# A streaming attention decode kernel: wq in two halves, the last unit in one transfer, wo in other parts

## The chip, the cores and the metric

The kernel runs on one core of a Trainium2 chip. The metric is the device time of one execution in microseconds (us), as the median of several runs. TensorE is PE (PEld: its weight loads), VectorE is DVE, ScalarE is ACT, GpSimd is POOL, SyncE is SP. Nearly all transfers are issued by SP, on one queue that 16 DMA engines serve.

## The reference

```python
# x: 2 x 1 x 448;  k_cache, v_cache: 2 x 16 x 4096 x 256;  wq: 448 x 4096;  wo: 4096 x 448
g = sigmoid((x * gate_w).sum(-1, keepdims=True))
q = (x @ wq) as (B, H, 1, Dh)
p = softmax(einsum("bhqd,bhkd->bhqk", q, k_cache) * Dh ** -0.5)
a = einsum("bhqk,bhkd->bhqd", p, v_cache) as (B, 1, H * Dh) @ wo
b = relu(x @ w1) @ w2            # w1: 448 x 1792, w2: 1792 x 448
out = g * a + (1 - g) * b
```

One query token for each of two batch rows, 16 heads, 4096 cached keys: every byte of the two caches (268 MB in float32) is read once.

## The kernel before, in words

The caches are cut into 32 units, one for each pair of batch row and head. A unit is a tile of 128 partitions by 16384 floats (8 MB): its first half holds K, its second V. Three slots of that size (`slot`, in `ring`) hold units in turn, unit u in slot u % 3. The weights pass through the same slots: wq through slot 2 before unit 2 needs it, w1 and w2 through slot 2 and wo through slot 0 when the last units in them are done.

The order of all large transfers is written out by hand in `sync`. SP issues wq, unit 0 and unit 1; then, in a loop of 10 turns of three, it waits for one count of the semaphore `free` (`take`: wait, then subtract) and issues the next unit. PE gives the first count of `free` after both halves of the projection (so that slot 2 may be overwritten), DVE one for each unit that it is done with. The last unit, 31, is issued in two transfers by a branch on the loop's turn: K signals `land[1]`, V signals `late`. After the next two counts come w1 with w2, and wo in 7 transfers of 7, 7, 7, 4, 4, 2 and 1 chunks; a chunk is 128 x 448 floats, and each transfer has its own semaphore. ACT issues one small transfer, xg: x and the gate's weights.

PE (`tensor`) waits for POOL's gate sums and DVE's `sel`, then projects: `project` multiplies 16 tiles into `ph`, ACT scales it into `wide`, PE transposes it into `pt`, ACT copies it into `qt`. It does so twice, one half of wq at a time, written out by a Python loop, after one wait for all of wq. Then for each unit `scores` waits for its landing and for its query, and multiplies K into `ps`. DVE takes the maximum (L284), ACT the exponential (L263) and the next unit's query (L256), DVE multiplies V by the probabilities with an accumulated sum, 8 times (L290). DVE's loop has a branch that waits for `late` in its last turn. In that way PE's scores of one unit run while DVE works on V of the one before.

After unit 31 the tail follows: PE transposes the maxima and sums (L204, L205) and projects with w1 (L172 with `xo`), DVE and ACT make the weights of the softmax (L294 to L298), PE spreads them, DVE scales (L300) and spreads the outputs into `lhs` (L302, semaphore `ot`). PE then multiplies `lhs` with w2's 14 chunks and wo's first 25 into `acc` (L229), waiting for each part of wo where it begins; DVE copies `acc` out (L306), PE folds its four row groups into `z` (L233), and the last 7 chunks (`DIRECT`) are multiplied straight into `z` in four pieces each (L238). DVE copies `z` (L308) and SP sends it.

Of the kernel before, what the change touches and what calls it, by code (L numbers as in the profile page):

```python
# [8 lines left out]
P, HP = 128, 64  # L9
G = 4  # L10
R = P // G
SLOTS = 3
CW = 512
DIRECT = 7


def take(e, sem, n=1):
    e.wait_ge(sem, n)
    e.sem_inc(sem, -n)  # L19
# [7 lines left out]
def gated_mix_decode(nc, xg, kv, wq, w1, w2, wo, out):  # L27
    U, _, LEN = kv.shape
    KC, B = xg.shape[1], xg.shape[2] - 1
    KF = KC - 1  # L30
# [3 lines left out]
    T = DH // P  # L34
    J = DH // R
    S = LEN // (2 * T)
# [6 lines left out]
    RB = R // B  # L43
    NQ = H * DH // (G * CW)
    FG = NF * P // G
    WQ, W1 = wq.shape[1] // NQ, w1.shape[1] // 2
    SCALE = float(DH) ** -0.5
    assert NQ == 2 and U % SLOTS == 2

    def sbuf(name, *shape):  # L50
        return nc.alloc_sbuf_tensor(name, [*shape], F32).ap()
# [2 lines left out]
        return nc.alloc_psum_tensor(name, [P, n], F32).ap()  # L54

    WO = [NF]
    for n in (7, 7, 7, 4, 4, 2, 1):
        WO.append(WO[-1] + n)
    assert WO[-1] == N
    names = ["xg", "wq", "w1", "w2", *(f"wo{k}" for k in WO[1:]), *(f"land{s}" for s in range(SLOTS)), "late",  # L60
             "pool", "vec", "act", "const", "sel", "sums", "gate", "omg", "xo", "proj", "wide", "pt", "hr",
             "query", "score", "top", "prob", "free", "tr", "nb", "e4", "wb", "wp", "os", "po", "ot",
             "acc", "a", "z", "res", "out"]
    sem = {n: nc.alloc_semaphore(n) for n in names}
    land = [sem[f"land{s}"] for s in range(SLOTS)]
# [3 lines left out]
    slot = [ring[:, s * LEN:(s + 1) * LEN] for s in range(SLOTS)]  # L69
# [8 lines left out]
    xr = sbuf("xr", P, KC, R)  # L78
# [23 lines left out]
    def slab(s, lo, hi, rows=slice(0, P)):  # L102
        return ring[rows, s * LEN + lo:s * LEN + hi]

    def rows_of(c, half):
        return slice(0, P) if c < KF else slice(half * HP, (half + 1) * HP)

    def bring(e, dst, src, signal):
        e.dma_start(dst, src).then_inc(signal, 16)  # L109

    def sync(e):
        bring(e, slab(2, 0, NQ * WQ), wq, sem["wq"])
        for u in range(2):
            bring(e, slot[u], kv[u], land[u])
        with e.Fori(0, U // SLOTS) as i:
            for k in range(SLOTS):
                take(e, sem["free"])
                s = (k + 2) % SLOTS
                src = kv[bass.ds(i * SLOTS + (k + 2), 1)].rearrange("o p n -> (o p) n")
                if k < SLOTS - 1:  # L120
                    bring(e, slot[s], src, land[s])
                    continue
                with e.If(i == U // SLOTS - 1):
                    bring(e, slot[s][:, :T * S], src[:, :T * S], land[s])
                    bring(e, slot[s][:, T * S:], src[:, T * S:], sem["late"])
                with e.Else():
                    bring(e, slot[s], src, land[s])
        take(e, sem["free"])
        bring(e, slab(2, 0, W2), w1, sem["w1"])
        bring(e, slab(2, W2, W2 + NF * D), w2, sem["w2"])  # L130
        take(e, sem["free"])
        for lo, hi in zip(WO, WO[1:]):
            bring(e, slab(0, (lo - NF) * D, (hi - NF) * D), wo[:, (lo - NF) * D:(hi - NF) * D], sem[f"wo{hi}"])
        e.wait_ge(sem["res"], 1)
        bring(e, out, res, sem["out"])
        nums = [s.num for n, s in sem.items() if n != "out"]
        assert nums == list(range(nums[0], nums[0] + len(nums)))
        e.sem_clear(range(nums[0], nums[0] + len(nums)))
# [23 lines left out]
    def tensor(e):  # L162
        e.wait_ge(sem["sums"], 1)
        e.matmul(gp, ones, gs, start=True, stop=True).then_inc(sem["gate"], 1)  # L164
        e.wait_ge(sem["sel"], 1)

        def project(x, width, place):
            for c in range(KC):
                for g in range(G):
                    at, half = place(c, g)  # L170
                    r = rows_of(c, half)
                    m = e.matmul(ph[g * R:(g + 1) * R, :width], x[r, c], slab(2, at, at + width, r), start=c == 0,  # L172
                                 stop=c == KC - 1)
            m.then_inc(sem["proj"], 1)
            take(e, sem["wide"])
            for k in range(width // P):
                t = e.transpose(pt[:, k * P:(k + 1) * P], wide[:, k * P:(k + 1) * P], ident)  # L177
            return t

        def scores(s):  # L180
            take(e, land[s], 16)
            take(e, sem["query"])
            for c in range(SG // CW):
                for t in range(T):
                    for g in range(G):
                        at = t * S + g * SG + c * CW
                        m = e.matmul(ps[g * R:(g + 1) * R, c * CW:(c + 1) * CW],  # L187
                                     query[:, t:t + 1].to_broadcast([P, R]), slot[s][:, at:at + CW], start=t == 0,
                                     stop=t == T - 1)
                        if c == SG // CW - 1 and t == T - 1:  # L190
                            m.then_inc(sem["score"], 1)

        e.wait_ge(sem["wq"], 16)
        for i in range(NQ):
            t = project(xr, CW, lambda c, g: (i * WQ + (g * KF + c if c < KF else G * KF + g % 2) * CW, g // 2))
            t.then_inc(sem["pt"], 1)
        e.drain().then_inc(sem["free"], 1)
        with e.Fori(0, -(-U // SLOTS)) as i:
            for s in range(SLOTS - 1):
                scores(s)  # L200
            with e.If(i < U // SLOTS):
                scores(SLOTS - 1)
        take(e, sem["query"])
        e.transpose(tp[:U, :P], nm[:, :U], ident)  # L204
        e.transpose(tp[:U, P:2 * P], ls[:, :U], ident).then_inc(sem["tr"], 1)  # L205
        e.wait_ge(sem["xo"], 1)
        e.wait_ge(sem["w1"], 16)
        project(xo, FG, lambda c, g: (g % 2 * W1 + (g // 2 * KF + c if c < KF else 2 * KF) * FG, g // 2))
        for j in range(2):
            t = e.matmul(pt[j * HP:(j + 1) * HP, KF * P:FG], wide[:, KF * P:FG], ident[:, j * HP:(j + 1) * HP],  # L210
                         start=True, stop=True)
        t.then_inc(sem["pt"], 1)
        e.wait_ge(sem["wb"], 1)
        e.matmul(wp, wb.rearrange("u g r -> u (g r)"), ident[:U, :U], start=True, stop=True).then_inc(sem["wp"], 1)
        e.wait_ge(sem["os"], 1)
        for g in range(G):
            m = e.matmul(po[g * R:(g + 1) * R, :nu], sel, os.rearrange("p u j -> p (u j)")[:, g * nu:(g + 1) * nu],
                         start=True, stop=True)
        m.then_inc(sem["po"], 1)
        e.wait_ge(sem["hr"], 1)  # L220
        e.wait_ge(sem["w2"], 16)
        for k in range(N - DIRECT):
            if k == NF:
                e.wait_ge(sem["ot"], 1)
            if k in WO:
                e.wait_ge(sem[f"wo{WO[WO.index(k) + 1]}"], 16)
            g = k % G
            w = slab(2, W2 + k * D, W2 + (k + 1) * D) if k < NF else slab(0, (k - NF) * D, (k - NF + 1) * D)
            m = e.matmul(acc[g * R:(g + 1) * R], lhs[:, k], w, start=k < G, stop=k >= N - DIRECT - G)  # L229
        m.then_inc(sem["acc"], 1)  # L230
        e.wait_ge(sem["a"], 1)
        for g in range(G):
            e.matmul(z[g * R:(g + 1) * R], sel, a_sb[:, g * DG:(g + 1) * DG], start=True, stop=False)  # L233
        for k in range(N - DIRECT, N):
            if k in WO:
                e.wait_ge(sem[f"wo{WO[WO.index(k) + 1]}"], 16)
            for g in range(G):
                m = e.matmul(z[g * R:(g + 1) * R], lhs[:, k], slab(0, (k - NF) * D + g * DG, (k - NF) * D + (g + 1) * DG),  # L238
                             start=False, stop=k == N - 1)
        m.then_inc(sem["z"], 1)  # L240
# [38 lines left out]
    def vector(e):  # L279
        e.wait_ge(sem["const"], 1)  # L280
        e.tensor_reduce(sel, ident.rearrange("p (g r) -> p r g", g=G), axis=AX.X, op=ALU.add).then_inc(sem["sel"], 1)  # L281
        with e.Fori(0, U) as u:
            take(e, sem["score"], G)
            e.tensor_reduce(nm[:, bass.ds(u, 1)], ps, axis=AX.X, op=ALU.max, negate=True).then_inc(sem["top"], 1)  # L284
            take(e, sem["prob"])
            with e.If(u == U - 1):
                e.wait_ge(sem["late"], 16)
            for j in range(J):
                v = ring[:, bass.ds((u % SLOTS) * LEN + (T * S + j * SG), SG)]
                m = e.scalar_tensor_tensor(v, v, 1.0, prob, op0=ALU.mult, op1=ALU.mult,  # L290
                                           accum_out=ov[:, bass.ds(u, 1), j])
            m.then_inc(sem["free"], 1)
# [77 lines left out]
```

## Time and profile before

| what | us |
|---|---|
| median of 3 runs (lowest, highest) | 675.61 (675.5, 675.85) |
| the profiled execution | 675.75 |
| its span, first to last instruction | 674.4 |
| DVE busy in the span | 338.8 |
| PE busy in the span | 213.4 |
| ACT busy in the span | 60.1 |
| DMA engines, share of the span | 99.3% of 16 |
| bytes read | 289.54 MB, 429 GB/s over the span |

The span is what the timeline counts, from 0; the execution's time is 1.35 us more. The page divides the span into 40 slices of 16.9 us; in its rows a digit is a busy share in tenths. In a timeline row stand the start, the duration, the engine, the line, the operation, output and inputs, how many instructions were merged, and in brackets how long the engine was idle before and what ended that. `PEq L19`, `DVEq L19` or `ACTq L19` there means a wait in `take`. In a row of windows stand the stretch, its length, each engine's busy time with its count of instructions, the clock that PE was granted, the share of the DMA engines and their GB/s.

### The profile page before, as it was taken

Reading aid. Unit: us, or ns where it says so; the run is one execution under the profiler, and the core shown is the slowest. Engines: PE = TensorE matmul, PEld = TensorE weight load, DVE = VectorE, ACT = ScalarE, POOL = GpSimd, SP = SyncE. Lnnn points to the kernel's source line nnn. Section 1 sums busy time; section 2 is a strip of 40 time slices with the busy share of each in tenths; the row PEclk is TensorE's granted clock in tenths of the full one; section 3 lists DMA queues with packets and bytes.
Section 4 is the critical chain, followed back from the end, with each engine's and each line's share of the span. In section 5 each row is a group of like instructions: output and inputs, shape, how many; then the busy total and the mean of one; then the engine's idle time right before and its main releaser. Section 6 shows DMA issues by size and latency. Waiting matters only on the chain. (4 is left out here: it accounts for less than half of the span.)

```text
span 674.4 us, 4267 instructions
## 1 busy us (share of the span) xinstructions
PE 213.4 (32%) x1291; PEld 55.9 (8%) x1291; DVE 338.8 (50%) x554; ACT 60.1 (9%) x118; POOL 2.2 (0%) x14
## 2 busy tenths in 40 slices
PE   0633221333332123333321233333222333332455
PEld 0110000000000000000000000000000000000111
DVE  0006566544556664454656545455665544556670
ACT  0020001001000100100010010000001001000110
POOL 0100000000000000000000000000000000000000
PEclk9975567767655676776567676665567667655869
DMA  9999999999999999999999999999999999999997
GB/s 381 428 435 436 435 435 435 435 435 435 435 435 435 435 435 435 435 431 435 435 435 435 435 435 435 435 435 435 435 435 435 435 435 435 435 435 406 414 433 318
DMA packets 6483, 289.65 MB, mean 430 GB/s; under 512 B 976, under 2 KB 1104, under 8 KB 1488
## 3 DMA queue, kind: packets, MB, share of 16 engines
q1 hardware_dynamic: 6336, 289.60, 99.3%
q8 instruction: 3, 0.05, 0.0%
q10 hardware_dynamic: 144, 0.01, 0.0%
HBM read 289.54 MB, written 0.06 MB: 429 GB/s over the span
## 5 line engine op out<-in xcount | busy, mean ns | idle before, releaser
L290 DVE SCALAR_TENSOR_TENSOR ring<-ring,prob 128x1024 f32 x256 | 295.9, 1221 | 78.8 <-DVEq L19 78.8
L187 PE MATMUL ps<-ring,query 128*32 128x512 f32 x1024 | 183.7, 883 | 416.6 <-PEq L19 416.6
L284 DVE TENSOR_REDUCE nm<-ps 128x1024 f32 x32 | 39.2, 1225 | 215.2 <-DVEq L19 215.2
L187 PEld LDWEIGHTS ps<-ring,query 128*32 128x32 f32 x1024 | 46.5, 155 | 553.1 <-issue 553.1
L263 ACT ACTIVATE prob<-ps,nm 128x1024 f32<-128x1024 f32 x32 | 35.6, 1113 | 370.9 <-ACTq L19 370.7
L263 ACT ACT_TABLE_LOAD x11 | 14.1, 1283 | 180.3 <-ACTq L19 180.3
L290 DVE DVE_READ_ACCUMULATOR ring<-ring,prob x256 | 21.2, 83 | 0.0
L281 DVE TENSOR_REDUCE sel<-ident 128x32 f32<-128x128 f32 x1 | 0.4, 369 | 22.7 <-POOL ident L155 22.7
L229 PE MATMUL acc<-ring,lhs 128*32 128x448 f32 x78 | 9.2, 544 | 4.9 <-DMA ring<-in_wo 4.9
L172 PE MATMUL ph<-ring,xr 128*32 128x512 f32 (+1 forms) x64 | 9.2, 713 | 0.7 <-DVE sel L281 0.7
L164 PE MATMUL tp<-gs,ones 128*128 128x2 f32 x2 | 0.6, 364 | 21.8 <-POOL gs L150 21.8
L306 DVE COPY wide<-acc 128x448 f32<-128x448 f32 x1 | 0.6, 625 | 12.7 <-PE acc L229 12.7
L172 PE MATMUL ph<-ring,xo 128*32 128x448 f32 (+1 forms) x32 | 5.4, 826 | 3.8 <-DMA ring<-in_w 3.8
L256 ACT ACTIVATE query<-qt 128x2 f32 (+1 forms) x33 | 6.4, 193 | 0.0
L263 ACT ACTIVATION_READ_ACCUMULATOR prob<-ps,nm x32 | 6.2, 193 | 0.0
L229 PEld LDWEIGHTS acc<-ring,lhs 128*32 128x32 f32 x78 | 2.5, 109 | 10.8 <-DMA ring<-in_wo 7.3
L177 PE MATMUL pt<-ident,wide 128*128 128x128 f32 x11 | 1.8, 280 | 2.7 <-PEq L19 2.7
L204 PE MATMUL tp<-ident,nm 128*32 128x128 f32 x1 | 0.4, 370 | 7.1 <-PEq L19 7.1
L172 PEld LDWEIGHTS ph<-ring,xr 128*32 128x32 f32 (+1 forms) x64 | 1.9, 126 | 6.5 <-issue 5.7
L164 PEld LDWEIGHTS tp<-gs,ones 128*128 128x128 f32 x2 | 0.5, 312 | 21.8 <-POOL gs L150 21.8
L249 ACT ACTIVATE wide<-ph 128x512 f32<-128x512 f32 x2 | 1.2, 597 | 9.6 <-ACTq L19 9.6
L238 PE MATMUL z<-ring,lhs 128*32 128x112 f32 x56 | 1.9, 264 | 0.1
(43 smaller groups left out, 15.2 us busy)
## 6 DMA issues: line engine op xcount, KB each, us to landing
ring<-in_kv SPq DMA_DIRECT2D x2, 4096.0 KB, 33.5
ring<-in_wq SPq DMA_DIRECT2D x1, 7168.0 KB, 19.6
ring<-in_w SPq DMA_DIRECT2D x2, 3136.0 KB, 29.9
ring<-in_wo SPq DMA_DIRECT2D x3, 1568.0 KB, 21.9
ring<-in_wo SPq DMA_DIRECT2D x2, 896.0 KB, 27.7
ring<-in_kv SPq DMA_DIRECT2D x31, 38.3
ring<-in_wo SPq DMA_DIRECT2D x1, 448.0 KB, 29.1
ring<-in_wo SPq DMA_DIRECT2D x1, 224.0 KB, 29.2
```

Of the source, the lines that this page charges most:

```text
L164: e.matmul(gp, ones, gs, start=True, stop=True).then_inc(sem["gate"], 1)
L172: m = e.matmul(ph[g * R:(g + 1) * R, :width], x[r, c], slab(2, at, at + width, r), start=c == 0, stop=c == KC - 1)
L177: t = e.transpose(pt[:, k * P:(k + 1) * P], wide[:, k * P:(k + 1) * P], ident)
L187: m = e.matmul(ps[g * R:(g + 1) * R, c * CW:(c + 1) * CW], query[:, t:t + 1].to_broadcast([P, R]), slot[s][:, at:at + CW], start=t == 0, s ...
L229: m = e.matmul(acc[g * R:(g + 1) * R], lhs[:, k], w, start=k < G, stop=k >= N - DIRECT - G)
L238: m = e.matmul(z[g * R:(g + 1) * R], lhs[:, k], slab(0, (k - NF) * D + g * DG, (k - NF) * D + (g + 1) * DG), start=False, stop=k == N - 1)
L249: e.activation(wide, ph, AF.Copy, scale=SCALE).then_inc(sem["wide"], 1)
L256: e.activation(query, qt[:, :, bass.ds(u, 1)].rearrange("p t o -> p (t o)"), AF.Copy).then_inc(sem["query"], 1)
L263: e.activation(prob, ps, AF.Exp, bias=nm[:, bass.ds(u, 1)], accum_out=ls[:, bass.ds(u, 1)]).then_inc(sem["prob"], 1)
L284: e.tensor_reduce(nm[:, bass.ds(u, 1)], ps, axis=AX.X, op=ALU.max, negate=True).then_inc(sem["top"], 1)
L290: m = e.scalar_tensor_tensor(v, v, 1.0, prob, op0=ALU.mult, op1=ALU.mult, accum_out=ov[:, bass.ds(u, 1), j])
L306: e.tensor_copy(a_sb, acc).then_inc(sem["a"], 1)
```

## The change

wq arrives as an array of two halves. Both are brought to the same place in slot 2: the first before unit 0, the second, after a count of `free`, before unit 1. PE's two projections become a loop of two turns on the chip, each of which waits for its half and gives a count of `free` after a drain. The last unit comes in one transfer like all others, so the branch in SP's loop, the branch in DVE's loop and the semaphore `late` go. wo comes in parts of 9, 9, 5, 3, 3, 2 and 1 chunks, of which the last 6 chunks, not 7, go straight into `z`.

```diff
-DIRECT = 7
+DIRECT = 6
...
-    WQ, W1 = wq.shape[1] // NQ, w1.shape[1] // 2
+    WQ, W1 = wq.shape[2], w1.shape[1] // 2
...
-    for n in (7, 7, 7, 4, 4, 2, 1):
+    for n in (9, 9, 5, 3, 3, 2, 1):
...
     def sync(e):
-        bring(e, slab(2, 0, NQ * WQ), wq, sem["wq"])
-        for u in range(2):
+        for u in range(NQ):
+            if u:
+                take(e, sem["free"])
+            bring(e, slab(2, 0, WQ), wq[u], sem["wq"])
             bring(e, slot[u], kv[u], land[u])
         with e.Fori(0, U // SLOTS) as i:
             for k in range(SLOTS):
                 take(e, sem["free"])
                 s = (k + 2) % SLOTS
                 src = kv[bass.ds(i * SLOTS + (k + 2), 1)].rearrange("o p n -> (o p) n")
-                if k < SLOTS - 1:
-                    bring(e, slot[s], src, land[s])
-                    continue
-                with e.If(i == U // SLOTS - 1):
-                    bring(e, slot[s][:, :T * S], src[:, :T * S], land[s])
-                    bring(e, slot[s][:, T * S:], src[:, T * S:], sem["late"])
-                with e.Else():
-                    bring(e, slot[s], src, land[s])
+                bring(e, slot[s], src, land[s])
...
-        e.wait_ge(sem["wq"], 16)
-        for i in range(NQ):
-            t = project(xr, CW, lambda c, g: (i * WQ + (g * KF + c if c < KF else G * KF + g % 2) * CW, g // 2))
+        with e.Fori(0, NQ):
+            take(e, sem["wq"], 16)
+            t = project(xr, CW, lambda c, g: ((g * KF + c if c < KF else G * KF + g % 2) * CW, g // 2))
             t.then_inc(sem["pt"], 1)
-        e.drain().then_inc(sem["free"], 1)
+            e.drain().then_inc(sem["free"], 1)
...
             take(e, sem["prob"])
-            with e.If(u == U - 1):
-                e.wait_ge(sem["late"], 16)
             for j in range(J):
...
-    wq = np.concatenate([full, last], 2).transpose(1, 0, 2).reshape(P, -1)
+    wq = np.concatenate([full, last], 2)
```

More of the change, by code (lines that the diff above doesn't have):

```diff
@@ L56, in gated_mix_decode @@
     WO = [NF]
-    for n in (7, 7, 7, 4, 4, 2, 1):
+    for n in (9, 9, 5, 3, 3, 2, 1):
         WO.append(WO[-1] + n)
     assert WO[-1] == N
-    names = ["xg", "wq", "w1", "w2", *(f"wo{k}" for k in WO[1:]), *(f"land{s}" for s in range(SLOTS)), "late",
+    names = ["xg", "wq", "w1", "w2", *(f"wo{k}" for k in WO[1:]), *(f"land{s}" for s in range(SLOTS)),
              "pool", "vec", "act", "const", "sel", "sums", "gate", "omg", "xo", "proj", "wide", "pt", "hr",
```

## The prediction

> **What bounds the kernel now.** I read the page's first lines first, then the chain that ended last.
>
> ```profile
> span 674.4 us, 4267 instructions
> ...
> DMA  9999999999999999999999999999999999999997
> GB/s 381 428 435 436 435 435 435 435 435 435 435 435 435 435 435 435 435 431 435 435 435 435 435 435 435 435 435 435 435 435 435 435 435 435 435 435 406 414 433 318
> ...
> q1 hardware_dynamic: 6336, 289.60, 99.3%
> q8 instruction: 3, 0.05, 0.0%
> ...
> DMA ring<-in_wo 4%; SPq L109 0%; PE z L238 0%; DVE res L308 0%
> ```
>
> The reader is to see one resource, full from first slice to last. 289.6 MB at 435 GB/s are 665.7 us of the 674.4; what is left is a start, a tail of about 3 us and a few dips. The chain, in order of time, ends with:
>
> ```profile
> 642.27 29.09 DMA ring<-in_wo
> ...
> 671.41 1.00 PE z L238 x24
> ...
> 672.44 0.28 DVE res L308
> ```
>
> So the time is "when does the last byte of wo land", plus 3 us. The change moves no byte out of the stream. It can cost only by (a) letting the queue run dry, or (b) making the last compute later than the last byte; it can gain only at the edges. I go through the places in that order.
>
> **The change at the start.** The timeline of the first 40 us, and two issue rows:
>
> ```profile
> 0.75 0.39 SPq L109 DMA_DIRECT2D ring<-in_wq  x1
> ...
> 20.59 0.20 POOL L146 TENSOR_TENSOR pg<-xg_sb 128x8 f32<-128x8 f32 x1 [19.61 <-DMA xg_sb<-in_xg]
> ...
> 23.15 5.46 PE L172 MATMUL ph<-ring,xr 128*32 128x512 f32 x32 [0.72 <-DVE sel L281]
> ...
> 30.07 3.77 PE L172 MATMUL ph<-ring,xr 128*32 128x512 f32 x32
> ...
> 34.75 0.63 PE L177 MATMUL pt<-ident,wide 128*128 128x128 f32 x4 [0.90 <-PEq L19]
> ...
> 39.93 5.47 PE L187 MATMUL ps<-ring,query 128*32 128x512 f32 x32 [4.56 <-PEq L19]
> ```
>
> ```profile
> ring<-in_wq SPq DMA_DIRECT2D x1, 7168.0 KB, 19.6
> ...
> out<-res SPq DMA_DIRECT2D x1, 56.0 KB, 1.6
> xg_sb<-in_xg ACTq DMA_DIRECT2D x1, 6.0 KB, 19.8
> ```
>
> Now SP issues wq (7168 KB), unit 0 and unit 1 at once. After the change it issues half of wq and unit 0, waits for PE's first turn, then issues the other half and unit 1. Behind that wait stand every later transfer on SP's queue, so the question is whether the order comes before unit 0 has drained. The 6 KB of xg take 19.8 us because they land together with wq, with which they were issued; PE's start (23.15) follows them by 2.6 us. Half of wq is 3.67 MB, 8.4 us less at 435 GB/s, so xg comes at about 12.2 and PE starts at 14.7. A turn took 7.0 us (23.15 to 30.07, where the next begins); turn 1 ends at 21.8. Issue to landing of the smallest transfer is 1.6 us, so the second half can flow by about 23.8. Half of wq and unit 0 have landed at 39.93 less 8.4, 31.5. The margin is some 7 us. If xg came no earlier than today, turn 1 would end at 30.2, the order could flow at 31.8, and the queue would be dry for 0.3 to, counting its own landing delay, 1.1 us. I take 0, as the row that gives 19.8 beside 19.6 ties xg to wq; 1.1 us is kept for the range.
>
> The second half lands when wq and unit 0 had both landed before, at 39.9, since the bytes ahead are the same. Turn 2 takes 7.0 us, to 46.9, and its "free" lets unit 2 be issued, needed only when unit 1 has landed:
>
> ```profile
> 59.26 6.05 PE L187 MATMUL ps<-ring,query 128*32 128x512 f32 x32 [13.85 <-PEq L19]
> 79.57 6.13 PE L187 MATMUL ps<-ring,query 128*32 128x512 f32 x32 [14.27 <-PEq L19]
> 98.88 5.01 PE L187 MATMUL ps<-ring,query 128*32 128x512 f32 x32 [13.18 <-PEq L19]
> ...
> 601.14 6.46 PE L187 MATMUL ps<-ring,query 128*32 128x512 f32 x32 [13.43 <-PEq L19]
> 620.41 5.37 PE L187 MATMUL ps<-ring,query 128*32 128x512 f32 x32 [12.81 <-PEq L19]
> 630.29 5.34 PE L187 MATMUL ps<-ring,query 128*32 128x512 f32 x32 [4.51 <-PEq L19]
> ```
>
> Unit 1 lands at 59.26: 12 us to spare. Unit 0's scores start about 7 us later than now (47 for 39.93). Each unit lands 19.3 us after the last and PE idles 13 to 14 us before each, so the delay is absorbed in one or two units; slot 0 is needed again only when unit 2 has landed (79.57), and unit 0 is done at about 47 + 20. Cost of the two-turn loop, its drain and its wait: 0, covered by those 12 us; without that cover it would be the 7 us of a turn.
>
> **One transfer for the last unit, one branch less.** The bytes and their rate stay: in halves, 8.39 MB of unit 31 and the 3.21 MB of w1 took from 620.41 to 647.08, 435 GB/s, as whole units do. One transfer fewer here and one more for wq cancel. SP's branch goes, unseen behind a queue that is a unit ahead. What changes is when unit 31's compute runs. The tail:
>
> ```profile
> 607.96 1.22 DVE L284 TENSOR_REDUCE nm<-ps 128x1024 f32 x1 [7.40 <-DVEq L19]
> ...
> 611.20 1.23 DVE L290 SCALAR_TENSOR_TENSOR ring<-ring,prob 128x1024 f32 x1 [2.02 <-DVEq L19]
> ...
> 620.37 0.08 DVE L290 DVE_READ_ACCUMULATOR ring<-ring,prob  x1
> ...
> 647.08 5.39 PE L172 MATMUL ph<-ring,xo 128*32 128x448 f32 x32 [3.80 <-DMA ring<-in_w]
> ...
> 652.33 0.14 DVE L294 TENSOR_REDUCE nb<-tp 32x1 f32<-32x4 f32 x1
> ...
> 655.10 4.80 PE L229 MATMUL acc<-ring,lhs 128*32 128x448 f32 x42
> 655.35 1.23 DVE L302 TENSOR_TENSOR lhs<-po,gate 128x1024 f32<-128x1024 f32 x1 [0.44 <-PE po L217]
> ...
> 662.36 1.70 PE L229 MATMUL acc<-ring,lhs 128*32 128x448 f32 x14 [2.45 <-DMA ring<-in_wo]
> ...
> 666.08 1.71 PE L229 MATMUL acc<-ring,lhs 128*32 128x448 f32 x14 [2.02 <-DMA ring<-in_wo]
> ...
> 668.20 0.96 PE L229 MATMUL acc<-ring,lhs 128*32 128x448 f32 x8 [0.41 <-DMA ring<-in_wo]
> ...
> 670.35 2.02 PE L238 MATMUL z<-ring,lhs 128*32 128x112 f32 x56
> ```
>
> Before, unit 31's scores start at 630.29 on its first half and DVE is through at 652.33. After, they wait for the whole unit, 620.41 + 19.3 = 639.7. From the start of scores to DVE's end unit 29 needed 601.14 to 620.37, 19.2 us, with scores of 6.46; scores vary from 5.01 to 6.46, so 17.8 to 19.2. The branch that DVE no longer takes lies in the idle 2.02 ahead of 611.20, of which the exponential and its accumulator read take 1.3; that leaves 0 to 0.5, and I take 0.2. DVE is through at 657.3 to 658.7: **5.0 to 6.4 us later**. Behind it the same steps follow (652.33 to acc's start at 655.10 is 2.8, to the end of L302 at 656.58 is 4.25): acc starts at 660.1 to 661.5, and its wo products may start at 661.6 to 663.0.
>
> Is that still hidden? acc now has 14 w2 chunks and 26 of wo, two instructions each, 80 in all. At full clock 14 instructions took 1.70 with the last one's tail and 8 took 0.96, so one costs about 0.1: 80 take 7.5 to 8 us, and acc could end at 668 to 669.5. The data set their own end: wo flows at 7 chunks in 3.72 us (662.36 to 666.08), 0.53 a chunk, and the last 6 chunks land in the 3.2 us ahead of the end. With the last chunk at about 672.0, as now, the last part of acc (the second 3) lands at 668.8 and is done by 669.5. From the end of acc to the direct products took 1.2 (669.16 to 670.35), and 48 direct instructions cost about 1.1 (56 took 2.02, waits for data included). That gives 671.8; the last chunk's own 8 end at 672.4. So there is slack of 0.6: acc may end at 670.1 unseen. At full clock the later unit is **covered, with about 0.6 us to spare**.
>
> **The clock takes that away.** PE's gap is new: its xo projection, which ended at 652.5, waits for unit 31's query now and so ends about 1.5 us later, near 654; then PE waits for DVE at 657.3 to 658.7 and for ACT behind that: 4 to 4.5 us idle. The trace has such a gap, 625.78 to 630.29:
>
> ```profile
> 624.00:627.00 3.00, 1.78 (x20) 0.28 (x11) 0.87 (x1) 0.00 (x0) 0.00 (x0) 1.00 0.83 360
> 627.00:630.00 3.00, 0.00 (x0) 0.00 (x0) 0.35 (x1) 2.44 (x4) 0.00 (x0) 1.00 1.19 513
> 630.00:633.00 3.00, 2.71 (x16) 0.92 (x20) 2.34 (x5) 0.14 (x2) 0.00 (x0) 0.63 0.81 350
> ```
>
> In these rows the granted clock (third number from the end) falls from 1.00 to 0.63 right after it. What a burst that starts cold costs is read from the scores: 5.01 to 6.46, where the 32 equal instructions at 30.07, in full clock, took 3.77: 1.2 to 2.7 us more. Cold, acc ends at 669.2 to 672.2 instead of 668 to 669.5. Beyond 670.1 each microsecond is one of time: 0 to 1.7 and, at the far corner, 2.1; in the middle 0.3 to 0.6. Warm it is 0. I take +0.3.
>
> The Trainium skill ("TensorE: Matmul & The Clock Gate", Part 1: The HAM clock gate) states that the clock halves after at least one idle window of about 3.4 us and that the windows run free of the kernel. By that rule a gap of 4 to 4.5 us would hold a whole idle window in about a quarter of the phases, so PE would mostly stay warm and the sum would be 0; the row above cooled after a gap of that length, and I give cold the larger weight.
>
> **wo in 9, 9, 5, 3, 3, 2, 1 with six direct.** Seven transfers stay seven, the last two (2, 1) are unchanged, so the tail after the last byte stays: 0. The coarser first parts land later (second at 18 chunks instead of 14), but PE is late anyway and finds both landed. One chunk moved from direct to acc lengthens acc by 0.2 and shortens the direct part by 8 short instructions (0.2); both are in the sums above.
>
> **Sum.** Start 0 (0 to +1.1), last unit and acc +0.3 (0 to +2.1), wo parts 0, instruction blocks (below) 0 (-1.0 to +1.0). The profiled execution took 675.75 us, its span 674.4; the runs' median is 675.61. So 674.4 becomes 674.7, and 675.61 becomes 675.9.
>
> **Rivals.**
> 1. *Cold acc decides outright* (slower). Place: acc, the sum's third term. It passes 0.2% (1.35 us, about what a measurement can tell from no change) when acc ends after 671.5, which needs the late end of both ranges. Time 677.0 to 677.7. For: the 0.63. Against: only the corner of the ranges gets there. 10%.
> 2. *The queue runs dry at the start* (slower). If xg is not earlier, +0.3 to +1.1: 675.9 to 676.7, with the cold acc added up to 677.5. Against: 19.8 beside 19.6. 6%.
> 3. *Instruction blocks move* (faster). The trace has 3 instruction packets, 0.05 MB, some 16 KB each. Scores 1 to 2 stand 20.31 apart where others are 19.31 apart: if each of the 16 engines carries an equal share of a transfer, one that fetches code loses 1.0 us and never catches up. The changed PE program is some 70 instructions shorter (32 matmuls with their loads and 4 transposes with theirs, less a loop). If one packet that now delays the last engine falls behind the last byte, up to 1.0 us is won, if two do, 2.0: 673.6 to 675.2. If two fall on one engine, 1.0 is lost. 16% for the gain, a third of it beyond 1.35 us.
>    The Trainium skill ("Runtime: NRT & Kernel Launch", Instruction fetch mechanics) states that code comes in 16 KiB blocks of 256 instructions and calls a crossing mostly hidden; by it this rival is 0, and the 20.31 is the only row here that speaks against.
> 4. *The change does nothing to the end*: PE stays warm, all cover holds, 675.5 to 675.7. 18%.
>
> **Chances.** The forecast (acc partly cold, 675.6 to 676.9) has 50%. Within 0.2% (674.3 to 677.0) lie the forecast but for its upper edge (47), rival 4 (18), two thirds of rival 3 (11) and half of rival 2 (3): 79%. Slower: rival 1 (10), the rest of rival 2 (3) and the forecast's edge (3): 16%. Faster: the rest of rival 3, 5%. The range 674.7 to 677.2 leaves out the far ends of rivals 1, 2 and 3.
>
> **What would show it.** Right: SP's second wq issue near 22 and no dip below 428 GB/s in the second slice; PE's first projection near 15; unit 31's scores near 639.7; L294 at 657 to 659; a PE clock under 1.00 somewhere in 656 to 666; acc without waits for the first two wo parts; the direct products ending within 1 us of 672.4. Wrong: a dip at 30 us, acc ending after 671.5, or a last wo landing that itself moves by over 0.5 us, which no compute step explains.

## The result and the profile after

The changed kernel's median is 677.11 us (22 runs, 675.61 to 678.10), that of the kernel before 675.79 beside it (22 runs): ratio 1.0017, 95% interval 1.001 to 1.0023. The medians are 1.3 us apart, and the ratio gives 1.2: a loss that is real, but inside the 0.2% that the prediction called no change. The profiled execution took 677.01 us, its span 675.7, 1.3 more than before. The page of the changed kernel (line numbers are those of its own file: L167 projects, L182 scores, L224 is acc, L228 and L233 are z, L287 is nb, L301 res):

```profile
span 675.7 us, 4217 instructions
...
GB/s 404 409 429 435 436 435 435 435 435 435 435 435 435 435 435 435 435 435 435 435 435 435 435 435 435 435 435 435 435 435 435 435 435 435 435 435 435 422 421 287
...
q8 instruction: 2, 0.03, 0.0%
...
PE acc L224 1%; PE z L233 0%; PE pt L172 0%; DVE wide L299 0%; PE tp L209 0%; PE po L212 0%; DVE os L293 0%; PE pt L205 0%; PE z L228 0%; DVE res L301 0%
```

The last line is the answer in short: the chain that ended last no longer holds a transfer. It is PE and DVE from the transposes ahead of the softmax weights (659.55) to the end. Its last part in order of time, and the timeline of the tail:

```profile
661.95 0.44 PE po L212 x8
662.39 9.08 PE acc L224 x80
671.47 0.02 issue
671.49 0.64 DVE wide L299
672.13 0.04 issue
672.17 0.40 PE z L228 x8
672.57 1.20 PE z L233 x48
```

```profile
640.02 5.99 PE L182 MATMUL ps<-ring,query 128*32 128x512 f32 x32 [13.92 <-PEq L19]
...
649.76 5.89 PE L167 MATMUL ph<-ring,xo 128*32 128x448 f32 x32
...
658.59 0.14 DVE L287 TENSOR_REDUCE nb<-tp 32x1 f32<-32x4 f32 x1
...
662.17 9.25 PE L224 MATMUL acc<-ring,lhs 128*32 128x448 f32 x80
```

Unit 31's scores now begin at 640.02 instead of 630.29; DVE is through at 658.59 instead of 652.33; acc is one run of 80 products with no wait for wo, from 662.17 to 671.47, where before it had waits in it and ended at 669.16. In windows, the clock (third number from the end) says what acc ran at:

```profile
652.00:655.00 3.00, 3.00 (x20) 0.59 (x16) 3.00 (x5) 0.00 (x0) 0.00 (x0) 0.50 0.98 420
655.00:658.00 3.00, 0.66 (x8) 0.00 (x0) 3.00 (x7) 0.00 (x0) 0.00 (x0) 0.99 1.00 430
658.00:661.00 3.00, 1.41 (x8) 0.99 (x9) 1.32 (x7) 0.68 (x2) 0.00 (x0) 0.58 1.00 430
661.00:664.00 3.00, 2.49 (x22) 1.10 (x26) 1.65 (x2) 0.55 (x1) 0.00 (x0) 0.50 0.96 406
664.00:667.00 3.00, 3.00 (x28) 0.87 (x24) 0.00 (x0) 0.00 (x0) 0.00 (x0) 0.78 1.00 415
667.00:670.00 3.00, 3.00 (x36) 0.96 (x32) 0.00 (x0) 0.00 (x0) 0.00 (x0) 1.00 1.00 406
```

PE had just come to full clock at 655 when its work ran out (the xo projection ends at 655.65), and when it resumed at 659.59 it was at 0.50 again, until about 665.

At the start, nothing was lost:

```profile
14.94 6.34 PE L167 MATMUL ph<-ring,xr 128*32 128x512 f32 x32 [0.91 <-PEq L19]
...
39.87 5.83 PE L167 MATMUL ph<-ring,xr 128*32 128x512 f32 x32 [17.07 <-PEq L19]
...
59.32 6.21 PE L182 MATMUL ps<-ring,query 128*32 128x512 f32 x32 [7.56 <-PEq L19]
78.81 5.01 PE L182 MATMUL ps<-ring,query 128*32 128x512 f32 x32 [13.28 <-PEq L19]
99.19 5.06 PE L182 MATMUL ps<-ring,query 128*32 128x512 f32 x32 [15.37 <-PEq L19]
```

```profile
22.95 0.33 SPq L109 DMA_DIRECT2D ring<-in_wq  x1
```

```profile
xg_sb<-in_xg ACTq DMA_DIRECT2D x1, 6.0 KB, 11.4
```

Unit 1 lands where it did (59.32 for 59.26), so the queue was never dry. One step between units is a microsecond too long. Before it stood between 59.26 and 79.57 (20.31 us), now between 78.81 and 99.19 (20.38): it came one unit later, and the trace's records of the instruction packet moved with it, from 63.0 to 82.6, which fits a program that is shorter ahead of PE's loop.

### The profile page after: what moved, and what is told of

The parts are those of the page before. It is cut to its first block, busy times and chain, and to the rows that moved or that the text cites. A ratio compares the mean times of both kernels' runs of the same rounds, so it can differ in the third digit from the quotient of the medians.

```text
span 675.7 us, 4217 instructions
## 1 busy us (share of the span) xinstructions
PE 216.7 (32%) x1285; PEld 57.2 (8%) x1285; DVE 338.9 (50%) x554; ACT 60.1 (9%) x118; POOL 2.2 (0%) x14
## 5 line engine op out<-in xcount | busy, mean ns | idle before, releaser
L182 PE MATMUL ps<-ring,query 128*32 128x512 f32 x1024 | 183.5, 882 | 415.3 <-PEq L19 415.3
L182 PEld LDWEIGHTS ps<-ring,query 128*32 128x32 f32 x1024 | 46.5, 155 | 551.6 <-issue 551.6
L167 PE MATMUL ph<-ring,xr 128*32 128x512 f32 (+1 forms) x64 | 12.2, 911 | 18.0 <-PEq L19 18.0
L224 PE MATMUL acc<-ring,lhs 128*32 128x448 f32 x80 | 9.2, 625 | 0.0
L167 PE MATMUL ph<-ring,xo 128*32 128x448 f32 (+1 forms) x32 | 5.9, 891 | 0.0
L167 PEld LDWEIGHTS ph<-ring,xr 128*32 128x32 f32 (+1 forms) x64 | 2.6, 150 | 26.1 <-issue 26.1
L224 PEld LDWEIGHTS acc<-ring,lhs 128*32 128x32 f32 x80 | 2.8, 128 | 5.8 <-issue 5.8
L167 PEld LDWEIGHTS ph<-ring,xo 128*32 128x32 f32 (+1 forms) x32 | 1.2, 158 | 4.1 <-issue 4.1
```

The costliest lines, as they stand in the source:

```text
L182: m = e.matmul(ps[g * R:(g + 1) * R, c * CW:(c + 1) * CW], query[:, t:t + 1].to_broadcast([P, R]), slot[s][:, at:at + CW], start=t == 0, s ...
```

## The experiments

Theory: unit 31's compute, moved 6 us later by the single transfer, uncovers the tail, and PE's gap before acc, which costs it its clock, does the rest. Rivals: the start (S), the coarser wo parts (W), lateness alone without the clock (L). All runs are timed beside the kernel before (675.65 to 675.88 in the four sets).

**1. The changed kernel, unit 31 in two transfers again.**

```diff
+                if k < SLOTS - 1:
+                    bring(e, slot[s], src, land[s])
+                    continue
+                with e.If(i == U // SLOTS - 1):
+                    bring(e, slot[s][:, :T * S], src[:, :T * S], land[s])
+                    bring(e, slot[s][:, T * S:], src[:, T * S:], sem["late"])
+                with e.Else():
+                    bring(e, slot[s], src, land[s])
...
+            with e.If(u == U - 1):
+                e.wait_ge(sem["late"], 16)
```

> The changed kernel with unit 31 in two transfers again (both branches and late are back); wq in halves and wo in 9, 9, 5, 3, 3, 2, 1 stay. Theory (unit 31 is computed 6 us later and its acc runs partly at half clock): all of the loss goes, 675.6 to 675.9, the chain ends in the transfer of wo again, and acc starts near 655. Rival W (the coarser wo parts cost it) and rival S (the start does): 676.9 to 677.3, as the changed kernel.

675.61 us (11 runs, 675.30 to 675.90), ratio 0.9993 (0.9984 to 1.0002). The whole loss is gone, acc starts at 655.30, and as the start and the wo parts are still changed here, neither S nor W can hold it.

**2. The kernel before, with unit 31 in one transfer** (the same lines the other way).

> The kernel before with unit 31 in one transfer and without both branches; wq whole, wo in 7, 7, 7, 4, 4, 2, 1. Theory: the whole loss is here, 676.5 to 677.5, and the chain ends in acc on PE. Rivals W and S: 675.6 to 675.9.

677.25 us (676.13 to 677.80), ratio 1.0018 (1.0009 to 1.0027). This part alone makes the whole loss; the chain ends in acc on PE.

**3. The changed kernel with the old wo parts** (7, 7, 7, 4, 4, 2, 1 and DIRECT = 7).

> The changed kernel with wo in 7, 7, 7, 4, 4, 2, 1 and seven direct chunks. Theory: acc ends 0.2 to 0.4 us earlier (one chunk less) and the direct part is one chunk longer, so within 0.2 us of the changed kernel, 676.8 to 677.3. Rival W: 675.7, as before.

677.69 us (676.35 to 678.23), ratio 1.0021 (1.0012 to 1.003). No better than the changed kernel, a little above the expected band, and its interval overlaps the changed kernel's. W fails here.

**4. The changed kernel with PE kept busy in the gap.**

```diff
-        def project(x, width, place):
+        def project(x, width, place, fill=0):
...
             m.then_inc(sem["proj"], 1)
+            for f in range(fill):
+                g = f % G
+                e.matmul(ps[g * R:(g + 1) * R, :CW], query[:, :1].to_broadcast([P, R]), slot[1][:, :CW], start=True,
+                         stop=True)
...
+        project(xo, FG, lambda c, g: (g % 2 * W1 + (g // 2 * KF + c if c < KF else 2 * KF) * FG, g // 2), fill=13)
```

> The changed kernel with 13 products of no use on PE between the xo projection and its transposes, into a bank that is read no more, so that PE is busy for 2.8 us (at full clock) of its 3.9 us of waiting for DVE. Theory: PE keeps full clock, acc ends at about 669.5 instead of 671.5 though it starts no earlier, 675.6 to 676.0, and the spread of single runs (675.6 to 678.1 in the changed kernel) shrinks to under 1 us. Rival L (the lateness alone does it, the clock does not matter): 676.9 to 677.3. If the projection itself ends cold, the products take up to 5.5 us and cost up to 1.6 us in some runs.

676.08 us (675.62 to 677.09), ratio 0.9999 (0.9981 to 1.0017). That interval is wide and overlaps the changed kernel's (1.001 to 1.0023). The runs of the same set are clearer: 10 of the 11 of experiment 3 are above 676.7, 9 of the 11 here are at 676.6 or below. Windows of this run, and rows of its timeline:

```profile
655.00:658.00 3.00, 3.00 (x32) 0.79 (x25) 3.00 (x7) 0.00 (x0) 0.00 (x0) 1.00 1.00 430
658.00:661.00 3.00, 2.14 (x15) 0.91 (x10) 1.54 (x8) 1.22 (x3) 0.00 (x0) 1.00 1.00 430
661.00:664.00 3.00, 2.96 (x40) 1.28 (x44) 1.23 (x1) 0.00 (x0) 0.00 (x0) 1.00 0.99 422
```

```profile
655.40 3.62 PE L172 MATMUL ps<-ring,query 128*32 128x512 f32 x26
...
658.40 0.14 DVE L291 TENSOR_REDUCE nb<-tp 32x1 f32<-32x4 f32 x1
...
661.17 8.41 PE L228 MATMUL acc<-ring,lhs 128*32 128x448 f32 x80
...
670.53 1.71 PE L237 MATMUL z<-ring,lhs 128*32 128x112 f32 x48
```

DVE is only 0.2 us earlier than in the changed kernel (658.40 for 658.59), yet acc begins 1.0 us earlier: the other 0.8 come from the small products ahead of it, which run at full clock too. acc takes 8.41, its waits for wo included, for 9.25, and ends at 669.58, inside the 670.1 that the prediction allowed. So L fails: adding useless work took away about 1 us, and the loss needs both, the lateness and the clock.

Two limits. The useless products also make PE's program 52 instructions longer, and this run has 3 instruction packets where the changed kernel has 2. Length is not what gained the time in the trace, as the changed kernel's chain holds no transfer and its out took 1.6 us; but no run put the same instructions elsewhere. And the spread (1.5 us) shrank less than expected. By the packet records the third packet ends at 673.3, 0.2 us ahead of the first bytes of out, so the longer runs may have met what experiment 8 shows below; none of them was traced.

**5. The start alone** (the kernel before with wq in halves and the loop of two turns).

> The kernel before with the start alone changed: wq in two halves into one place, PE in a loop of two turns; unit 31 in two transfers, wo in 7, 7, 7, 4, 4, 2, 1. Theory (the loss is the late unit 31 and its acc at half clock): 675.6 to 675.9, second order for wq near 23 us. A rival that holds part of the loss at the start: 676.1 or more.

675.91 us (675.51 to 677.50, two of 11 runs at 677.5), ratio 1.0002 (0.9993 to 1.0011). No cost; S fails. What the two runs met is open.

**6. DVE later: the changed kernel with two more passes after unit 31.**

```diff
+        for j in range(2):
+            v = ring[:, LEN + j * SG:LEN + (j + 1) * SG]
+            e.scalar_tensor_tensor(v, v, 1.0, prob, op0=ALU.mult, op1=ALU.mult, accum_out=res[:, j:j + 1])
         e.wait_ge(sem["tr"], 1)
```

> The changed kernel with two more passes on DVE after unit 31's, over K that is read no more, their sums unused: DVE reaches L287 2.3 us later. Theory: past the slack every microsecond counts, and PE's gap of 6.2 us now always holds a whole idle window, so the time is 2.3 us above the slower runs of the changed kernel: 679.0 to 680.0, spread under 1.5 us. Rival (something other than the late end of unit 31 sets the loss, and acc has cover left): 677.0 to 678.0.

680.38 us (5 runs, 679.11 to 681.26), ratio 1.0067 (1.0053 to 1.0081): 3.3 us over the changed kernel for 2.3 us of work. There is no cover left, as expected. Size and spread came out above the band, and acc took longer (9.84 for 9.25). PE's gap was 6.19 us and its clock did fall in it; that such a gap always cools PE is more than one trace shows.

```profile
664.43 9.84 PE L224 MATMUL acc<-ring,lhs 128*32 128x448 f32 x80
```

**7. DVE earlier: the changed kernel with 4 passes over V for unit 31** (`attend(U - 1, ..., J // 2)` behind the loop, which now runs to U - 1). It leaves out half of unit 31's output, so it stands for the time alone.

> The changed kernel with 4 instead of 8 passes over V for unit 31 (half of that unit's output is left out and filled from unit 30); the last unit still comes in one transfer, with the changed start and wo parts. DVE reaches L287 4.5 us earlier, near 654. Theory: it is the lateness, not the form of the transfer: 675.5 to 675.9, chain back in the transfer of wo. Rival (the single transfer itself is slower, or hurts what comes behind it): 676.8 to 677.3.

675.57 us (675.36 to 676.20), ratio 0.9999 (0.999 to 1.0008). With the transfer still in one piece and DVE through at 654.15 instead of 658.59, the loss is gone. The form of the transfer costs nothing; what waits for it does.

**8. The wo parts alone, twice, and what follows from them** (the kernel before with 9, 9, 5, 3, 3, 2, 1 and six direct chunks).

> The kernel before with wo alone in 9, 9, 5, 3, 3, 2, 1 and six direct chunks. Theory: 675.6 to 675.9, acc waits for its parts and PE may lose its clock between them, but acc ends by 670. A rival that holds part of the loss in the coarser parts: 676.1 or more.

> The kernel before with wo alone in 9, 9, 5, 3, 3, 2, 1, a second time and beside the next one. If the cost of the parts is real: 676.3 to 677.0 with single runs up to 677.6. If the first time was chance: 675.6 to 675.9.

676.67 us (675.47 to 677.63), ratio 1.0013 (1.0004 to 1.0022), and again 676.13 (675.37 to 677.48), ratio 1.0008 (0.9999 to 1.0017). A miss: here the parts do cost, in some runs, by 1 to 2 us. Beside the second of these, experiment 1's kernel, which has the same parts, ran once more:

> The changed kernel with unit 31 in two transfers, a second time: it has the same coarse parts and was 675.61. If the coarse parts cost in every such kernel, this time some runs come out at 676.5 to 677.6; if the changed start protects it, 675.5 to 675.8 again.

675.59 us (675.40 to 676.00), ratio 1.0 (0.9991 to 1.0009). So it is not the parts as such. My first guess was the clock again, now in the gaps between the coarser parts, and I filled them:

```diff
         for k in range(N - DIRECT):
             if k == NF:
                 e.wait_ge(sem["ot"], 1)
+            for f in range({NF: 7, WO[1]: 8}.get(k, 0)):
+                e.matmul(ps[f % G * R:(f % G + 1) * R, :CW], query[:, :1].to_broadcast([P, R]), slot[1][:, :CW],
+                         start=True, stop=True)
```

> The kernel before with wo in 9, 9, 5, 3, 3, 2, 1 and six direct chunks (676.67 alone), and 7 and 8 products of no use on PE ahead of its waits for the first two parts, which fill most of its gaps of 1.9 and 2.3 us there. Theory C (the coarser parts cost through the clock: a gap of 2.3 us in a window of 3.4 us lets PE fall to half clock in some runs, and the rest of acc is late): 675.6 to 675.9, no run above 676.5 but those that the kernel before has too. Rival F (the cost of the coarser parts lies elsewhere, in the transfers or the code fetch): as without them, 676.3 to 677.0.

675.63 us (675.35 to 676.04), ratio 0.9997 (0.9988 to 1.0006): as theory C said. But the profile of the second run of the wo parts had caught one of its long executions (677.24 us), and it speaks against C. Its windows of the tail, its order for out, its instruction packets with out's time to landing, and the same two rows of the first run's profile (an execution of 675.83 us):

```profile
660.00:663.00 3.00, 2.54 (x26) 1.10 (x18) 0.00 (x0) 0.00 (x0) 0.00 (x0) 1.00 0.95 406
663.00:666.00 3.00, 1.34 (x16) 0.53 (x17) 0.00 (x0) 0.00 (x0) 0.00 (x0) 1.00 1.00 419
666.00:669.00 3.00, 2.77 (x19) 0.57 (x17) 0.00 (x0) 0.00 (x0) 0.00 (x0) 1.00 1.01 418
669.00:672.00 3.00, 2.24 (x55) 1.15 (x54) 0.62 (x1) 0.00 (x0) 0.00 (x0) 1.00 0.36 140
```

```profile
672.94 0.35 SPq L109 DMA_DIRECT2D out<-res  x1
```

```profile
q8 instruction: 3, 0.05, 0.0%
...
out<-res SPq DMA_DIRECT2D x1, 56.0 KB, 3.0
```

```profile
q8 instruction: 2, 0.03, 0.0%
...
out<-res SPq DMA_DIRECT2D x1, 56.0 KB, 1.6
```

The clock is 1.00 in these rows and out is issued at 672.94, within 0.4 us of the short executions (from 655 to 661 the clock was 0.70 and 0.73, but acc then waits 2.12 us for wo, and the short execution of the last run below was as cold there). It is out itself that takes 3.0 us instead of 1.6, in the execution that has a third instruction packet. In the trace's packet records that packet runs from 673.63 to 674.86, just ahead of the bytes of out, and the last packets of out begin at 674.84; in the kernel before it begins at 671.6, and the shorter execution has none. The fill of theory C had also made PE's program 60 instructions longer, so its result did not tell the two apart. The last run has the longer program without the fill near the end:

```diff
         e.drain().then_inc(sem["free"], 1)
+        for f in range(15):
+            e.matmul(ps[f % G * R:(f % G + 1) * R, :P], ones[:, :R], ident, start=True, stop=True)
         with e.Fori(0, -(-U // SLOTS)) as i:
```

> The kernel before with wo alone in 9, 9, 5, 3, 3, 2, 1 and six direct chunks (676.67 and 676.13 alone), and 15 products of no use at 36 us, where PE waits for unit 0: they lengthen PE's program by 60 instructions, as the products of the run with PE kept busy between the parts did (675.63), but do nothing to PE's clock near the end. Theory B (an instruction packet that comes only after the last byte of wo stands in front of the 56 KB of out in some runs, 3.0 us for 1.6; a longer program asks for it earlier): 675.5 to 675.9, no run above 676.5, three instruction packets. Theory C (the clock between the coarser parts): 676.1 to 676.7 with runs up to 677.5, as without the padding.

675.64 us (675.22 to 676.16), ratio 0.9997 (0.9988 to 1.0006), three instruction packets, out in 1.6 us, no run above 676.2. The clock from 655 to 661 was 0.61 and 0.82. The longer program also moved the first packet, from 63.0 to 46.0, and the step that is a microsecond too long went with it (units at 40.01 and 60.20, 20.19 us apart).

Theory B is borne out: that loss was a matter of program length, not of the parts. The profiles fit it. The kernels with a PE program at least as long as the kernel before (experiment 2 and the two padded ones) have 3 packets; the parts alone, 12 instructions shorter, have 2 in one execution and 3 in the other; the changed kernel and experiments 1, 3, 5, 6 and 7, shortened by the loop, have 2. Experiment 4, with the loop and 52 instructions more, has 3, the last one late (672.3). The changed kernel does not show the loss in its profiled execution (out in 1.6 us). What stays open is that only one long execution was traced, and that the last run was timed without the unpadded kernel beside it.

No version beat the kernel before by more than its interval; the best (experiment 1 and the two padded kernels of experiment 8) are level with it.

## Why the prediction was right or wrong, point by point

- *The bound and the direction*: right. The end is the last byte of wo plus 3 us unless a late compute passes it; here it did.
- *The forecast and rival 1*: by its time the result is rival 1's and not the forecast's. The 677.11 lies in its 677.0 to 677.7 (10%) and above the 675.6 to 676.9 that had 50%, and acc ended at 671.47, at the edge of the 671.5 that rival 1 named. That the loss still stayed within 0.2% (0.17), and the median 0.1 us inside the range, is in part luck.
- *Start, 0*: right, by experiments 1 and 5. xg came when half of wq did (PE's first projection at 14.94, foretold 14.7), SP's second order at 22.95, against a need at 31.5. One of the signs that I named was badly chosen: the second slice fell to 409 GB/s, below the 428 that I had set, while the first rose from 381 to 404; unit 1's landing shows that nothing was dry. Rival 2 did not come.
- *Unit 31 later by 5.0 to 6.4 us*: right, 658.59 less 652.33 is 6.26, near the late end, with scores of 5.99. The last bytes of wo did not move (671.6 by the packet records, before and after), but the direct products ended at 673.72, 1.3 past the 672.4 that I had named as a sign.
- *The slack, acc may end at 670.1*: right to 0.1. In the changed kernel acc ended 1.37 past it and the span grew by 1.3; with PE kept busy it ended at 669.58, and the span was 674.4 as before.
- *The clock*: right as mechanism (0.58 and 0.50 from 658 to 664, and experiment 4). **The size of this term was the step that failed.** I took +0.3, from 0.3 to 0.6 in the middle of the cold case and 0 in the warm one; the medians are 1.3 apart. acc itself was within what I had allowed: 9.25 for 7.5 to 8 at full clock, 1.3 to 1.8 more, against 1.2 to 2.7. Two things were missing in the term. The small products ahead of acc also ran cold (0.87 for 0.52 and 0.63 for 0.40 below, before and after), so acc started at 662.17 and not at 660.1 to 661.5. And the cold case seems to be not one among several but the usual one: 20 of 22 runs are above 676.0, for 5 of 22 before, and acc is cold in the profiles of experiments 2, 3 and 6 as well (9.15, 9.29 and 9.84); the clock of the other runs was not traced. My gap was not added up rightly either: from 654 to 1.0 us behind a DVE end of 657.3 to 658.7 are 4.3 to 5.7 us, not 4 to 4.5. It was 3.94, as the xo projection ended at 655.65.

```profile
653.33 0.52 PE L177 MATMUL pt<-ident,wide 128*128 128x128 f32 x3 [0.86 <-PEq L19]
...
654.05 0.40 PE L214 MATMUL tp<-ident,wb 32*128 32x32 f32 x2
```

```profile
659.59 0.87 PE L172 MATMUL pt<-ident,wide 128*128 128x128 f32 x3 [3.94 <-PEq L19]
...
660.81 0.63 PE L209 MATMUL tp<-ident,wb 32*128 32x32 f32 x2
```

- *Rival 4 (PE stays warm)*, and with it the Trainium skill's rule ("TensorE: Matmul & The Clock Gate", Part 1: The HAM clock gate) read strictly, where only a wholly idle window halves the clock: did not come true as the usual case. The row 655 to 658 has PE busy for 0.66 of 3 us and the clock fell right behind it. The trace agrees with the Trainium skill there in that full clock came back after sustained work, at about 665. The traces of before and after show how little idle time is enough. By their clock records the clock changes in steps of 3.41 us. PE fell to 0.50 after such steps in which it was busy for up to 41% of the time and stayed at 1.00 after those with 42% or more; the step from 655.06 to 658.47 had 17%. (In the other traces the border lies at 41 to 43%, but four of them have one fall after 58%, in the tail among small products.) So a gap of about 2 us, an estimate from 58% of 3.41, can cool PE where it falls into one step.
- *wo parts, 0*: right for the change as a whole (3 and both runs of 1). As an edit alone it cost about 0.1%, by a cause that I had looked for elsewhere.
- *Rival 3 (instruction blocks)*: the blocks did move (20.31 to 20.38, one unit later; 3 packets to 2), and the time did not follow: experiment 1, with 2 packets, is level with the kernel before, with 3. A packet still falls in the stream of wo (by the packet records at 666.1, for 657.2 before), which may be why; that was not tested. Where it decided was a place that I had not named, ahead of out, in experiment 8. The Trainium skill ("Runtime: NRT & Kernel Launch", Instruction fetch mechanics) calls such a crossing mostly hidden; here it was not in two places: 1.0 us on a unit's landing, and 1.4 us on out.

## What to carry to other kernels

In a kernel that is bound by its transfers, ask of every merge of transfers what compute waits for the merged one, and compare its end with the last byte: here 6 us of cover were spent to save a branch, and about 0.6 us were left to pay for the rest. Where PE must sprint at the end, look at the gap ahead of it: here 3.9 us without work left PE at half clock from 659.6 to about 665, and useless products in the gap gave back about 1 us. When an edit changes a program's length, its time can move by a microsecond for that alone, as in experiment 8, and an experiment that adds instructions needs a run that adds them elsewhere. Experiment 4 has no such run and rests on its trace.

## What the runs showed that was not expected

A transfer of 56 KB took 3.0 us instead of 1.6 with one 16 KB instruction packet ahead of it, at the very end where nothing covers it. And the changed kernel's runs spread over 2.5 us (675.61 to 678.10), where all but one of the kernel before lie within 0.9. The Trainium skill ("TensorE: Matmul & The Clock Gate", Part 1: The HAM clock gate) states that the windows of the clock run free of the kernel, so that a gap would meet them differently in each run. That fits, but was not measured run by run, and no trace of a fast run of the changed kernel (675.61, 675.94) was kept.
